# Bias of a spectral layer written into a PSUM bank by ScalarE; one copy in place of two for the inverse stage

## The chip, the cores and the metric

The kernel runs on one core of a Trainium2 chip. The metric is the device time of one launch in microseconds (us). Engines are named as in the profile: PE is TensorE's matmul, PEld its weight load, DVE is VectorE, ACT is ScalarE, POOL is GpSimd, SP is the engine that issues most DMAs.

## The reference, cut to what matters

Eight sequences of 2496 rows by 256 columns go through a spectral layer, and the result, 19968 tokens, through a top-1 mixture of eight experts.

```python
X = np.fft.rfft(x, axis=1)
Yr = Xr @ w_r - Xi @ w_i + b_r
Yi = Xr @ w_i + Xi @ w_r + b_i
Yr = np.sign(Yr) * np.maximum(np.abs(Yr) - lam, 0.0)     # Yi the same
y = np.fft.irfft(Yr + 1j * Yi, n=2496, axis=1)
...
expert_idx = np.argmax(y @ w_gate, axis=1)
ye = np.maximum(xe @ w1[e], 0.0) @ w2[e]
out = gate_w * ye          # softmax weight of the chosen expert
```

## The kernel before, in words

The transform of 2496 points is done in two factors, 39 and 64. Of the 39 columns of frequencies only 20 are needed (k1 = 0 to 19), and two of them make a slot, so a sequence has 10 slots and the eight sequences 80. A slot goes through the following steps; each is a method of the class.

- `fwd_a` (L295) does the first factor for a whole sequence: products into a bank (`pa`), a copy to `ae`, a DMA to a scratch in DRAM. `turn` (L310) reads a slot back with the axes turned.
- `fwd_b` (L317) does the second factor of one slot into the bank `pb`; `halves` (L327) splits the result into a high and a low part, `sh` and `sl`, and their sum. ACT does `re` (L334), `sh` (L335) and the `sh` of the sum (L339).
- `mix` (L343) is the complex product with w_r + i w_i as three real products of six matmuls each. The first of the three goes to the bank `pk`, and ACT copies it to `k` (L357). After a `yield` the other two go to the two halves of one bank, `pm`, which has a single buffer: first a bf16 matmul of ones with the three-way split bias (L361, 512 columns, `start=True`), then twice six products (L351) onto it. DVE adds `k` to both halves and writes `v` (L365).
- `shrink` (L369) is the soft threshold: ACT writes `r` (L373), DVE `y` (L379).
- `inv_b` (L386) does the first factor of the inverse: four fp32 products, each of two instructions in the trace, into the bank `pv`, and two ACT copies (L396) that scatter it into `z`, one per half of the 256 columns. `z` holds for each of 64 rows 40 numbers next to each other, four of them per slot.
- `inv_a` (L399) does the other factor, in groups: `pz`, the split `zh` and `zl`, `py`, and a copy to `yb`. `route` (L588) chooses the expert and scatters the rows to DRAM, as generators that `tick` steps on, mostly short DVE work.

The loop over the slots is in `spectral` (L423). In the slot loop the order on PE, SP, ACT and DVE is the order in which the code is written (`manual_schedule`); before the loop PE and SP are in written order, and ACT and DVE are ordered by a planner. Each engine takes its instructions strictly in order. In slot `it` the loop issues `fwd_b` and `halves` of the next slot, `shrink` of the last, and `mix` of this one. In slots 2 to 5 of a sequence other than the first ("turning" slots) it also issues `inv_a` of the sequence before; in the other slots `inv_b`. What stands ahead of `k` on ACT differs: in slots that are not turning, of sequences 0 to 6, it is `re`, `sh`, `r`, the `sh` of the sum and the two `z` copies; in turning slots `zh` and `ae` in place of the `z` copies; in the last sequence (`late`) the first half of `mix` is issued ahead of the `z` copies.

`pk` and `py` share a pool tag (`yo`) with two buffers, so a later `py` waits until ACT has copied `k`. `load_bias` (L200) issues six small DMAs on POOL, `split_bias` (L276) splits them in three on DVE. `keep_warm` (L543) issues products of zeros. After the loop come the last sequence's `inv_a`, and then the experts, which take the larger part of the time.

Of the kernel before, what the change touches and what calls it, by code (L numbers as in the profile page):

```python
# [10 lines left out]
F32 = mybir.dt.float32  # L11
# [9 lines left out]
NA, NB = 39, 64  # L21
# [3 lines left out]
D = 256  # L25
# [12 lines left out]
def constants(nb):  # L38
    n1 = np.arange(NA)
    n2 = np.arange(NB)  # L40
    k2 = np.arange(NB)
    fa = np.zeros((117, 120))
    fe = np.zeros((78, 120))
    ga = np.zeros((120, 117))
    for j in range(3):
        for k1 in range(K1):
            ph = 2 * np.pi * ((n1 * k1) % NA) / NA
            c, r = j * 40 + 2 * k1, slice(j * 39, (j + 1) * 39)
            for q, v in enumerate((np.cos(ph), -np.sin(ph))):
                fa[j::3, (2 * k1 + q) * 3 + j] = v  # L50
                if j < 2:
                    fe[j::2, (2 * k1 + q) * 3 + j] = v
            f = (1 if k1 == 0 else 2) / S
            ga[c, r] = f * np.cos(ph)
            ga[c + 1, r] = -f * np.sin(ph)
    bm = np.zeros((128, K1, 128))
    bi = np.zeros((128, K1, 128))
    for k1 in range(K1):
        k = k1 + NA * k2
        s = np.where(k > S // 2, -1.0, 1.0)  # L60
        th = 2 * np.pi * ((n2[:, None] * k[None, :]) % S) / S
        c, z = np.cos(th), np.sin(th)
        bm[:64, k1, :64] = c
        bm[64:, k1, :64] = z
        bm[:64, k1, 64:] = -z * s
        bm[64:, k1, 64:] = c * s
        live = (((k != 0) & (k != S // 2)) * s)[:, None]
        bi[:64, k1, :64] = c.T
        bi[64:, k1, :64] = -z.T * live
        bi[:64, k1, 64:] = z.T  # L70
        bi[64:, k1, 64:] = c.T * live
    cap = TT + nb * S
    nt = (nb * S + E * (TT - 1)) // TT
    p = np.arange(117)
    g = np.arange(G)
    n2o = p[:, None] // NA + 3 * g[None, :]
    tok = NB * (p[:, None] % NA) + n2o
    ok = n2o < NB
    ids = np.where(ok[:, None, :], tok[:, None, :] + S * np.arange(nb)[None, :, None], OOB)
    score = np.broadcast_to((8.0 - np.arange(E))[None, None, :], (117, G, E)) * ok[:, :, None]  # L80
    base = np.broadcast_to((np.arange(E) * cap + TT)[None, :], (128, E))
    ltri = (p[:, None] < p[None, :]).astype(np.float64)
    tcol = np.stack([np.arange(128.0), np.arange(128.0) - 1, np.where(np.arange(128) == 0, 1.0, 0.0),
                     np.arange(128.0), np.arange(128.0) + 128], 1)
    return {
        "c_fa": fa.astype(np.float32),
        "c_fe": fe.astype(np.float32),
        "c_ga": ga.astype(np.float32),
        "c_bm": bm.astype(np.float32),
        "c_bi": bi.astype(np.float32),  # L90
        "c_ids": np.ascontiguousarray(ids.astype(np.int32)),
        "c_score": np.ascontiguousarray(score.astype(np.float32)),
        "c_base": np.ascontiguousarray(base.astype(np.float32)),
        "c_ltri": ltri.astype(np.float32),
        "c_tcol": tcol.astype(np.float32),
    }


class Kernel:
# [243 lines left out]
    def mix(self, b, s):  # L343
        nc = self.nc
        sh, sl = self.ss.pop((b, s))

        def product(nm, slot, to, first=True, last=True):
            i = 0
            for c in range(2):
                for a, ww in ((sh, self.wh), (sh, self.wl), (sl, self.wh)):  # L350
                    nc.tensor.matmul(to, a[:, c, slot, :], ww[nm][:, c, :], start=first and i == 0, stop=last and i == 5)  # L351
                    i += 1

        pk = self.psi.tile([128, 512], F32, tag="yo", name="pk")
        product("r", 2, pk[:, :D])
        k = self.w.tile([128, D], F32, tag="k", name="k")
        nc.scalar.copy(k, pk[:, :D])  # L357
        self.mark_row(k)
        yield
        p = self.psf.tile([128, 2, D], F32, tag="m", name="pm", bufs=1)  # L360
        nc.tensor.matmul(p.rearrange("p r d -> p (r d)"), self.ones_b, self.bias3[:117], start=True, stop=False)  # L361
        product("d", 0, p[:, 1, :], False, False)
        product("s", 1, p[:, 0, :], False)
        u = self.w.tile([128, 2, D], F32, tag="v", name="v")
        nc.vector.tensor_add(u, p, k.unsqueeze(1).broadcast_to((128, 2, D)))  # L365
        self.mark_row(u)
        self.us[b, s] = u
# [18 lines left out]
    def inv_b(self, b, s):  # L386
        nc = self.nc
        y = self.ys.pop((b, s))
        p = self.psi.tile([128, 512], F32, tag="u", name="pv", bufs=4).rearrange(
            "p (c a r n) -> p c a r n", c=2, a=2, r=2)  # L390
        for kp in range(2):
            for c in range(2):
                nc.tensor.matmul(p[:, c, kp, :, :], y[:, kp, c * 128:(c + 1) * 128], self.bi[:, 2 * s + kp, :],
                                 start=True, stop=True)
        for c in range(2):
            nc.scalar.copy(self.z[:, c, 0:NB, 4 * s:4 * s + 4].rearrange("p n a -> p a n"),  # L396
                           p[:, c].rearrange("p a r n -> p (a r) n"))

    def inv_a(self, b, i):  # L399
        nc = self.nc  # L400
# [20 lines left out]
                self.jobs.append(self.route(b, g // GH, self.yb))  # L421

    def spectral(self, fwd):  # L423
        nb = self.nb
        self.t1s, self.pbs, self.ss, self.us, self.ys, self.hl = {}, {}, {}, {}, {}, {}
        self.jobs, self.rows = [], []
        pairs = [(q, g) for q in range(6) for g in ((0, 2) if q < 5 else (0,))]
# [1 line left out]
        n = len(todo)  # L429
        self.keep_warm(18)  # L430
        self.split_bias()
        for i in pairs:
            self.fwd_a(0, *i)
        self.load_weights()
# [16 lines left out]
        first, loads, back = ({i: [] for i in range(n)} for _ in range(3))  # L451
# [15 lines left out]
        for it in range(n):  # L467
            b, s = todo[it]
# [25 lines left out]
            if late and not turning:  # L494
                next(mix)
            if not turning:
                inverse()
            if not late and not turning:
                next(mix)
            for a in first[it]:  # L500
                self.fwd_a(*a)
            if turning:
                next(mix)
# [544 lines left out]
```

## Time and profile before

| | |
|---|---|
| median of 3 runs | 1521.19 us (1520.15 to 1521.5) |
| profiled execution, its own time | 1522.23 us |
| its span | 1520.4 us |
| busy, PE / DVE / ACT / POOL | 98% / 73% / 62% / 29% |
| slot loop | from 31 us to 573 us of the span |

Times in the profile are microseconds from the start of the span. A row of the timeline gives start, duration, engine, line, operation, what is written and read, and in brackets how long the engine had been idle and which engine released it. Matmuls overlap in the array, so the spacing of their starts, not their duration, is what one costs. Durations of ACT and DVE overlap the next one by about a tenth of a microsecond as well.

### The profile page before, as it was taken

The numbers are of one execution on the slowest core, as the hardware profiler recorded it, in microseconds if no ns is written. First come the engines' busy times: TensorE is split into PE (matmuls) and PEld (weight loads), VectorE is DVE, ScalarE is ACT, GpSimd is POOL, SyncE is SP. The second block draws the span as 40 slices with busy tenths as digits, with TensorE's granted clock in tenths as the row PEclk, the third lists the DMA queues.
The fourth block names the chain that finished last, engine by engine and source line by source line (L and its number), as shares of the span: only waits on it lengthen the run. The fifth ranks groups of instructions, "written<-read, shape, count | busy, mean of one in ns | idle before, by whom it ended". The sixth has DMA issues, their size and how long they took to land. (4 is left out here: it accounts for less than half of the span.)

```text
span 1520.4 us, 29861 instructions
## 1 busy us (share of the span) xinstructions
PE 1496.1 (98%) x9367; PEld 1313.4 (86%) x9367; DVE 1105.4 (73%) x2412; ACT 943.0 (62%) x2008; POOL 439.6 (29%) x527
## 2 busy tenths in 40 slices
PE   8999999999999999999999999999999999999997
PEld 4789899998989988888888888888888888998997
DVE  4678687777777987676766667666666666788885
ACT  2677777777777767455555555555555555676764
POOL 1101524435261635611221221122122112232232
PEclk9999999999999999999999999999999999999999
DMA  8953545546362314452232413322323243555421
GB/s 247 278 156 111 174 144 148 156 144 181 113 195 86 113 33 156 116 133 53 57 91 50 112 41 73 83 56 70 71 56 104 44 105 98 145 143 153 100 49 28
DMA packets 191518, 169.69 MB, mean 112 GB/s; under 512 B 117525, under 2 KB 159881, under 8 KB 191354
## 3 DMA queue, kind: packets, MB, share of 16 engines
q1 hardware_dynamic: 171390, 123.48, 31.9%
q0 software_dynamic: 19712, 43.75, 8.7%
q8 instruction: 76, 1.25, 0.4%
q14 instruction: 88, 0.72, 0.2%
q10 hardware_dynamic: 252, 0.50, 0.1%
HBM read 171.51 MB, written 66.37 MB: 156 GB/s over the span
## 5 line engine op out<-in xcount | busy, mean ns | idle before, releaser
L965 PE MATMUL po<-h,hh 128*128 128x512 f32 x1312 | 453.7, 393 | 0.0
L909 ACT ACTIVATE hh<-ph 128x512 fp32r<-128x512 f32 x328 | 196.1, 598 | 209.6 <-PE ph L904 189.2
L962 PE MATMUL po<-h,hl 128*128 128x256 f32 x1148 | 321.2, 280 | 0.0
L910 DVE SCALAR_TENSOR_TENSOR hl<-ph,hh 128x512 fp32r<-128x512 f32 x328 | 226.2, 691 | 125.8 <-ACT hh L909 117.9
L939 POOL DMA_INDIRECT out<-o,xr x116 | 139.3, 1201 | 501.1 <-DVE o L937 495.1
L904 PE MATMUL ph<-xh,l 128*128 128x512 f32 (+1 forms) x800 | 281.2, 351 | 1.0 <-DVE l L834 1.0
L904 PE MATMUL ph<-xh,h 128*128 128x512 f32 (+1 forms) x800 | 281.4, 352 | 0.3 <-ACT h L833 0.2
L904 PE MATMUL ph<-xl,h 128*128 128x512 f32 (+1 forms) x800 | 280.7, 351 | 0.0
L965 PEld LDWEIGHTS po<-h,hh 128*128 128x128 f32 x1312 | 238.4, 188 | 43.0 <-ACT hh L909 0.2
L962 PEld LDWEIGHTS po<-h,hl 128*128 128x128 f32 x1148 | 215.8, 188 | 6.0
L654 POOL DMA_INDIRECT xs_dram<-yb,pos x176 | 177.8, 1010 | 70.1 <-issue 35.3
L904 PEld LDWEIGHTS ph<-xh,l 128*128 128x128 f32 x800 | 151.3, 189 | 22.7 <-DVE l L834 1.6
L936 ACT ACTIVATE part<-po,xr 128x256 f32<-128x256 f32 x152 | 72.2, 475 | 156.5 <-PE po L965 156.5
L904 PEld LDWEIGHTS ph<-xl,h 128*128 128x128 f32 x800 | 151.3, 189 | 20.2
L904 PEld LDWEIGHTS ph<-xh,h 128*128 128x128 f32 x800 | 151.3, 189 | 19.9 <-ACT h L833 0.8
L937 DVE SCALAR_TENSOR_TENSOR o<-po,xr,part 128x256 f32<-128x256 f32 x152 | 73.3, 482 | 111.2 <-ACT part L936 108.9
L379 DVE SCALAR_TENSOR_TENSOR y<-v,r 64x256 f32<-64x256 f32 x320 | 133.8, 418 | 6.8 <-ACT r L373 1.6
L834 DVE TENSOR_TENSOR l<-r,h 128x512 fp32r<-128x512 f32 x200 | 128.1, 686 | 5.0 <-ACT h L833 3.5
L849 DVE TENSOR_TENSOR h<-r,h 128x512 fp32r<-128x512 f32 x200 | 127.8, 684 | 2.0 <-ACT h L848 1.3
L833 ACT CAST h<-r 128x512 fp32r<-128x512 f32 x200 | 112.2, 616 | 2.9 <-DMA r<-moe_w 2.8
L848 ACT CAST h<-r 128x512 fp32r<-128x512 f32 x200 | 112.3, 617 | 1.6 <-DMA r<-moe_w 1.6
L939 POOL DMA_INDIRECT out<-o,row x36 | 63.8, 1773 | 142.7 <-DVE o L937 136.6
(178 smaller groups left out, 2832.7 us busy)
## 6 DMA issues: line engine op xcount, KB each, us to landing
r<-moe_w SPq DMA_DIRECT2D x106, 512.0 KB
r<-moe_w SPq DMA_DIRECT2D x376, 128.0 KB
spec_dram<-ae SPq DMA_DIRECT2D x88, 240.0 KB
t<-spec_dram SPq DMA_DIRECT2D x160, 128.0 KB
x<-x SPq DMA_DIRECT2D x40, 384.0 KB
xq<-xs_dram SPq DMA_DIRECT2D x116, 128.0 KB
xq<-xs_dram SPq DMA_DIRECT2D x72, 64.0 KB
x<-x SPq DMA_DIRECT2D x35, 84.0 KB
```

Source lines behind the costliest of these rows:

```text
L379: nc.vector.scalar_tensor_tensor(out=y[q * 64:q * 64 + 64, kp, :], in0=u[h, q, :], scalar=LAM, in1=r[h, q, :], op0=ALU.add, op1=ALU.min)
L654: i = nc.gpsimd.indirect_dma_start(out=self.xs[:, :], out_offset=bass.IndirectOffsetOnAxis(ap=pos[:n, g:g + 1], axis=0), in_=y[:n, g, 0:XW ...
L833: nc.scalar.copy(hi[:, c, s], v)
L834: nc.vector.tensor_sub(lo[:, c, s], v, hi[:, c, s])
L848: nc.scalar.copy(hi[:, s, :], v)
L849: nc.vector.tensor_sub(lo[:, s, :], v, hi[:, s, :])
L904: nc.tensor.matmul(p[:, i, :], a[:, c, f * 128:(f + 1) * 128], v[:, c, :], start=m == 0, stop=m == 5)
L909: nc.scalar.activation(hh[:, s, :], p, AF.Relu)
L910: nc.vector.scalar_tensor_tensor(out=hl[:, s, :], in0=p, scalar=0.0, in1=hh[:, s, :], op0=ALU.max, op1=ALU.subtract)
L939: i = nc.gpsimd.indirect_dma_start(out=self.out[:, :], out_offset=bass.IndirectOffsetOnAxis(ap=at[h], axis=0), in_=o[:, h, :], in_offset=N ...
L962: nc.tensor.matmul(p[:, :D], hl[:, f - 1, hs], w2[:, f - 1, 0, :], start=False, stop=False)
L965: nc.tensor.matmul(p, hh[:, f, hs], w2[:, f].rearrange("p a d -> p (a d)"), start=f == 0, stop=f == 7)
```

## The change

The columns of the table `bi` are interleaved, so that `pv` can be laid out with the four numbers of a slot next to each other, and one ACT copy moves both halves into `z` in runs of four numbers (16 bytes). Each product of `inv_b` then writes its 128 columns as 64 pairs, with a gap of two numbers after each pair. The bias is summed once, ahead of the first `fwd_a`, by one matmul into the bank `pm` with `start=True`, and DVE copies it to a tile `biasf`. In each slot ACT copies `biasf` (128 x 512) into the bank `pm`, ahead of `k` on ACT, and all twelve products of the second half of `mix` add to it; none of them has `start=True`.

```diff
-        bi[:64, k1, :64] = c.T
-        bi[64:, k1, :64] = -z.T * live
-        bi[:64, k1, 64:] = z.T
-        bi[64:, k1, 64:] = c.T * live
+        bi[:64, k1, 0::2] = c.T
+        bi[64:, k1, 0::2] = -z.T * live
+        bi[:64, k1, 1::2] = z.T
+        bi[64:, k1, 1::2] = c.T * live
...
         product("r", 2, pk[:, :D])
+        p = self.psf.tile([128, 2, D], F32, tag="m", name="pm", bufs=1)
+        nc.scalar.copy(p.rearrange("p r d -> p (r d)"), self.biasf)
         k = self.w.tile([128, D], F32, tag="k", name="k")
         nc.scalar.copy(k, pk[:, :D])
         self.mark_row(k)
         yield
-        p = self.psf.tile([128, 2, D], F32, tag="m", name="pm", bufs=1)
-        nc.tensor.matmul(p.rearrange("p r d -> p (r d)"), self.ones_b, self.bias3[:117], start=True, stop=False)
         product("d", 0, p[:, 1, :], False, False)
         product("s", 1, p[:, 0, :], False)
...
-            "p (c a r n) -> p c a r n", c=2, a=2, r=2)
+            "p (c n a r) -> p c n a r", c=2, a=2, r=2)
         for kp in range(2):
             for c in range(2):
-                nc.tensor.matmul(p[:, c, kp, :, :], y[:, kp, c * 128:(c + 1) * 128], self.bi[:, 2 * s + kp, :],
+                nc.tensor.matmul(p[:, c, :, kp, :], y[:, kp, c * 128:(c + 1) * 128], self.bi[:, 2 * s + kp, :],
                                  start=True, stop=True)
-        for c in range(2):
-            nc.scalar.copy(self.z[:, c, 0:NB, 4 * s:4 * s + 4].rearrange("p n a -> p a n"),
-                           p[:, c].rearrange("p a r n -> p (a r) n"))
+        nc.scalar.copy(self.z[:, :, 0:NB, 4 * s:4 * s + 4], p.rearrange("p c n a r -> p c n (a r)"))
...
         self.keep_warm(18)
         self.split_bias()
+        p = self.psf.tile([128, 512], F32, tag="m", name="pm0", bufs=1)
+        nc.tensor.matmul(p, self.ones_b, self.bias3[:117], start=True, stop=True)
+        self.biasf = self.f.tile([128, 2 * D], F32, name="biasf")
+        nc.vector.tensor_copy(self.biasf, p)
         for i in pairs:
             self.fwd_a(0, *i)
```

## Rows read from the trace of the kernel before

**Rows 1.** The page, busy time by engine: us, share of the span, number of instructions.

```profile
PE 1496.1 (98%) x9367; PEld 1313.4 (86%) x9367; DVE 1105.4 (73%) x2412; ACT 943.0 (62%) x2008; POOL 439.6 (29%) x527
```

**Rows 2.** Busy time in one stretch, the last 13 slots of the loop: length, then busy us of PE, PEld, DVE, ACT, POOL with the instructions, granted clock, DMA share, GB/s.

```profile
485.00:572.00 87.00, 84.43 (x680) 79.39 (x680) 76.62 (x241) 61.71 (x148) 40.66 (x64) 1.00 0.27 80
```

**Rows 3.** What PE waited for from 30 to 600 us: waiting line, what released it, total us, times, longest.

```profile
PE pb L323 <- DMA t<-spec_dram: 1.6, 1, 1.6
...
PE py L418 <- ACT k L357: 0.8, 1, 0.8
```

**Rows 4.** Groups of instructions by line over the whole span: shapes, count, busy us, mean ns of one, idle before.

```profile
L833 ACT CAST h<-r 128x512 fp32r<-128x512 f32 x200 | 112.2, 616 | 2.9 <-DMA r<-moe_w 2.8
...
L396 ACT COPY z<-pv 128x256 f32<-128x256 f32 x160 | 92.9, 707 | 1.5 <-PE pv L393 1.5
...
L335 ACT CAST sh<-pb 128x512 fp32r<-128x512 f32 x80 | 47.4, 592 | 0.0
...
L361 PE MATMUL pm<-bias,ones_b 117*128 117x512 bf16 x80 | 30.9, 387 | 0.3 <-DVE v L365 0.3
```

**Rows 5.** Timeline of ACT in one slot, slot 1 of sequence 4, to the first row of the next slot.

```profile
302.76 0.37 ACT L334 COPY re<-pb 128x256 f32<-128x256 f32 x1 [1.84 <-PE pb L323]
303.03 0.59 ACT L335 CAST sh<-pb 128x512 fp32r<-128x512 f32 x1
303.51 0.74 ACT L373 ACTIVATE r<-v,nlam 128x512 f32<-128x512 f32 x1
...
304.43 1.17 ACT L396 COPY z<-pv 128x256 f32<-128x256 f32 x2
305.35 0.46 ACT L357 COPY k<-pk 128x256 f32<-128x256 f32 x1
...
307.76 0.37 ACT L334 COPY re<-pb 128x256 f32<-128x256 f32 x1 [1.48 <-PE pb L323]
```

**Rows 6.** Timeline of PE in the same slot: the bias product, and the second and third of the twelve products after it.

```profile
304.98 0.38 PE L361 MATMUL pm<-bias,ones_b 117*128 117x512 bf16 x1
...
305.31 0.28 PE L351 MATMUL pm<-wld,sh 128*128 128x256 f32 x1
305.43 0.28 PE L351 MATMUL pm<-whd,sl 128*128 128x256 f32 x1
```

**Rows 7.** Timeline, the bias product on PE and `k` on ACT in other slots that are not turning: slots 5 and 9 of sequence 0, slots 6 and 7 of sequence 3 (with the `pv` products of the latter), slot 0 of sequence 4.

```profile
61.37 0.46 ACT L357 COPY k<-pk 128x256 f32<-128x256 f32 x1
61.86 0.38 PE L361 MATMUL pm<-bias,ones_b 117*128 117x512 bf16 x1
...
83.95 0.38 PE L361 MATMUL pm<-bias,ones_b 117*128 117x512 bf16 x1
84.32 0.46 ACT L357 COPY k<-pk 128x256 f32<-128x256 f32 x1
...
275.60 0.45 ACT L357 COPY k<-pk 128x256 f32<-128x256 f32 x1
276.28 0.38 PE L361 MATMUL pm<-bias,ones_b 117*128 117x512 bf16 x1
...
281.27 1.05 PE L393 MATMUL pv<-bi,y 128*128 128x128 f32 x8
282.16 0.38 PE L361 MATMUL pm<-bias,ones_b 117*128 117x512 bf16 x1
282.88 0.45 ACT L357 COPY k<-pk 128x256 f32<-128x256 f32 x1
...
299.49 0.46 ACT L357 COPY k<-pk 128x256 f32<-128x256 f32 x1
299.98 0.38 PE L361 MATMUL pm<-bias,ones_b 117*128 117x512 bf16 x1
```

**Rows 8.** Timeline of a turning slot, slot 3 of sequence 4: `k` on ACT, the second `py` after it and the bias product on PE.

```profile
319.46 0.38 ACT L357 COPY k<-pk 128x256 f32<-128x256 f32 x1
...
320.45 0.29 PE L418 MATMUL py<-zh,gh 120*117 120x272 f32 x1
...
320.83 0.39 PE L361 MATMUL pm<-bias,ones_b 117*128 117x512 bf16 x1
```

**Rows 9.** Timeline: the bias product and `k` in slot 7 of sequence 6, and the bias product four slots later, in slot 1 of sequence 7.

```profile
490.28 0.38 PE L361 MATMUL pm<-bias,ones_b 117*128 117x512 bf16 x1
...
491.88 0.43 ACT L357 COPY k<-pk 128x256 f32<-128x256 f32 x1
...
509.43 0.38 PE L361 MATMUL pm<-bias,ones_b 117*128 117x512 bf16 x1
```

**Rows 10.** Timeline of the start: the last of POOL's six bias DMAs, the first products of `fwd_a`, SP's issues of `ae` to DRAM, the first round of the bias split on DVE, and the first reads of a slot.

```profile
5.37 0.48 POOL L205 DMA_DIRECT2D bias<-b_i  x1
...
7.73 3.60 PE L299 MATMUL pa<-x,far 117*120 117x512 f32 x8
...
11.04 8.73 SPq L308 DMA_DIRECT2D spec_dram<-ae  x11
...
14.56 0.41 DVE L281 CAST b<-bias 128x512 bf16<-128x512 f32 x1
...
15.21 0.67 DVE L284 TENSOR_TENSOR bias<-bias,b 128x512 f32<-128x512 f32 x1
...
22.80 2.57 SPq L314 DMA_DIRECT2D t<-spec_dram  x4
```

More of the change, by code (lines that the diff above doesn't have):

```diff
@@ L350, in product @@
                 for a, ww in ((sh, self.wh), (sh, self.wl), (sl, self.wh)):
-                    nc.tensor.matmul(to, a[:, c, slot, :], ww[nm][:, c, :], start=first and i == 0, stop=last and i == 5)
+                    nc.tensor.matmul(to, a[:, c, slot, :], ww[nm][:, c, :], start=first and i == 0, stop=last and i == 5,
+                                     skip_group_check=not first)
                     i += 1
@@ L423, in spectral @@
     def spectral(self, fwd):
-        nb = self.nb
+        nc, nb = self.nc, self.nb
         self.t1s, self.pbs, self.ss, self.us, self.ys, self.hl = {}, {}, {}, {}, {}, {}
```

## The prediction, as put on record

> **What bounds the kernel now.** I read the page's busy times first. PE is busy for 98% of the span [rows 1], so a saving on PE counts, and so does every wait that PE is given. Next I asked what PE waited for in the slot loop, since the change is made there: one wait for a DMA of 1.6 us, one of 0.8 us for `k`, and little else [rows 3]. So PE sets the time of the loop, and ACT and DVE follow it. Only the last 13 slots differ: there DVE is busy for 76.6 of 87.0 us [rows 2], and PE has little left over it. Last I read the timeline slot by slot for one question: how far is ACT behind PE at the point where the change makes PE wait for ACT?
>
> **What the edit takes from PE.** The bias product starts at 304.98 and the second of the twelve products at 305.31 [rows 6]; the third follows the second after 0.12 us, so the bias product costs 0.33 - 0.12 = 0.21 us. There are 80 [rows 4]: 16.8 us if nothing waits.
>
> **What it puts on ACT.** One copy of 128 x 512 from SBUF into PSUM. No row shows that direction. The nearest are 592 ns (PSUM to SBUF) and 616 ns (SBUF to SBUF) for the same shape [rows 4]; I take 0.60 us until it is done, with ends of 0.45 and 0.74 (`r`, [rows 5]). Until the next instruction can start I take 0.50 us (`sh` to `r` is 0.48 [rows 5]). The Trainium skill (page "ScalarE: Activation LUTs", section "Step-by-step: what each stage is for") says that ScalarE writes faster to PSUM than to SBUF; that would lower the 0.60, and no row here shows by how much.
>
> **What it takes from ACT.** Two `z` copies, of 0.707 us mean [rows 4], which together hold ACT from 304.43 to 305.35, 0.92 us [rows 5]. One copy of twice the size, four numbers at a time: I take the contiguous 128 x 512 rate, 0.48 us to the next start, since `k`, as large as one `z` copy and contiguous, takes 0.46 against 0.707. The other end is no gain, 0.92. ACT's total hardly changes (0.50 more, 0.44 less). Its order does matter.
>
> **The new wait.** The bias copy stands on ACT directly ahead of `k`, behind `z`, and PE's twelve products now wait for it. Behind them on PE are `pb` of the next slot, and so `re`, `sh` and everything after; ACT is idle 1.8 us before `re` and waits for `pb` [rows 5], so a slot that is late makes the next late by as much. Where two `z` copies stand ahead, `k` starts now at z + 0.92; the bias copy will start at z + 0.48 and end at z + 1.08, that is `k` + 0.16; with 0.06 us for the release, PE can go on at `k` + 0.22. Now I compare this, slot by slot, with the time at which PE reaches the bias product today:
>
> - Slot 1 of a sequence: 305.35 + 0.22 - 304.98 = 0.59 us late; less the 0.21 saved, 0.38 us lost [rows 5, 6]. Six sequences (1 to 6): +2.3.
> - Slot 7, where an exponential of the routing delays ACT: 282.88 + 0.22 - 282.16 = 0.94 late, 0.73 lost [rows 7]. Sequences 1 to 5: +3.65. Slot 8 is taken as even.
> - Slots 0, 6 and 9: 299.49 + 0.22 - 299.98 is negative, and so is 275.60 + 0.22 - 276.28 [rows 7]. No wait, 0.21 gained: 6 + 6 + 5 slots, -3.6.
> - Turning slots: the bias copy begins where `k` does, 319.46, and ends at 320.06; PE comes at 320.83 [rows 8]. 24 slots, -5.1. But `k` ends 0.50 later, at 320.34, and the `py` at 320.45 needs its bank: 0.05 us to spare, and none where `k` is late already, as in the one wait of 0.8 us [rows 3, 8]. I add 1.0, with ends 0 and 3.
> - Sequence 0: slots 2 to 5 gain (61.37 against 61.86), 7 to 9 lose 0.38 each (84.32 + 0.22 - 83.95 - 0.21) [rows 7]. The first slot loses about 1. What has gathered before slot 8 falls into the DMA wait of 1.6 us [rows 3]; slots 8 and 9 remain: +0.8.
>
> Sequences 1 to 6 come to 2.3 + 3.65 - 3.6 - 5.1 + 1.0 = -1.8.
>
> **The last slots.** From slot 7 of sequence 6 ACT is far behind PE, because `r` waits for DVE. That slot loses 491.88 + 0.22 - 490.28 - 0.21 = 1.6 us [rows 9]. After it a ring closes: bias copy, twelve products, `pb`, `re`, `sh`, `r`, `sh` of the sum, bias copy. From the products to the next `re` takes 307.76 - 304.98 - 0.21 = 2.57 us, from `re` to where `z` stands 1.67 [rows 5, 6], the bias copy with its release 0.66: 4.90 us, and 5.38 with a `z` copy ahead. Four slots, two of each kind, need 20.6 us; PE does them in 509.43 - 490.28 = 19.15 today [rows 9]. So 1.4 more, 3.0 with the first. Slots 2 to 6 of sequence 7 give back 5 x 0.21. In slots 7 to 9 DVE sets the pace [rows 2], and only the last bias copy shows, about +0.5. Together +2.5.
>
> **The start.** PE's order is the written one, and the new matmul `pm0` stands ahead of the first `fwd_a`. It needs the whole bias split, which DVE does today from 14.56 on, in between. The last bias DMA is issued at 5.85. When it lands no row tells: after 5.85 and before 14.56. By SP's writes, whose last issue ends at 19.77 and whose readers start at 22.80, 3.0 us from issue to landing: 8.9. Two rounds of 1.32 us (14.56 to 15.88) and a short third make 3.3 us: `pm0` at 12.2, where `fwd_a` begins at 7.73 today [rows 10]. That is 4.5 us later. Part of it comes back, since by then more of x has landed and the writes share the DMA engines with fewer loads. I take +2.5, with ends 0 and +9 (a landing at 14.56).
>
> **Sum.** -1.8 + 0.8 + 2.5 + 2.5 = +4.0 us on the profiled execution's 1522.2: 1526.2. It lies 1.0 above the median, so 1525 us for the median.
>
> **Rivals.**
> 1. *The copy is hidden and PE keeps its saving.* 80 x 0.21 less the start's 2.5: 1507 us. For it: ACT idles before every `re`. Against it: that idle time lies before `re`, and the copy is at the end of ACT's chain. It decides if `z` and the bias copy together take under 0.55 us in slot 1; I have 1.08. Chance 0.14.
> 2. *The single `z` copy costs as much as the pair.* Then the bias copy ends 0.44 us later: some 20 slots that already wait lose 8.8, the ten with a margin of 0.27 lose 0.17 each, the last slots about 1: +11.5, 1537 us. For it: no row has runs of four. Chance 0.12.
> 3. *The products of `inv_b` slow down*, because they write pairs with gaps. Today eight of them start 0.111 us apart (281.27 to 282.16 [rows 7]). At double the spacing, 640 x 0.111 = +71 us: 1596 us. No row has such an output. The Trainium skill speaks against the change here: "PSUM — Partial Sum Buffer", section "Specifications (TRN2)", says that any non-contiguous pattern slows matmuls significantly. [...] Chance 0.05.
> 4. *The start costs nothing*, because the bias lands early and the DMAs make up the rest: 1522.5 us, no difference. Chance 0.14.
>
> **How the numbers follow.** My forecast has 0.55. Within 0.2% (3 us, about what can be told from no change) lie 1518.2 to 1524.2. Of the 0.55 the larger part, 0.39, is slower, 0.13 the same, 0.03 faster. With the rivals: slower 0.39 + 0.12 + 0.05 = 0.56, the same 0.13 + 0.14 = 0.27, faster 0.17. The bounds of the bias copy (25 waiting slots by 0.15 us, 4 us) and of the start (-2.5 to +6.5) give the forecast its own range, 1518 to 1533. For 8 in 10 I take 1512 to 1540, which leaves out rival 3 and rival 1 in its full size.
>
> **What would show it.** Right: PE's list of waits has the products of `pm` released by ACT's `pm` copy, about 0.6 us in each slot 1 and 0.9 in each slot 7, none in slots 0, 6, 9 and in turning slots; `z` rows of about 0.6 us in one piece; the first `fwd_a` near 12 us and the first `pb` near 29. Wrong: a list of waits without ACT's copy, or `pv` products more than 0.111 us apart, or a first `fwd_a` still near 8 us.

## The result and the profile after

The changed kernel takes 1537.67 us (median of 4 runs, 1536.68 to 1540.2) against 1521.35 us for the kernel before on the same chip: ratio 1.0106, 95% interval 1.009 to 1.0122. It is slower by 16.3 us. The forecast was slower by about 4. The profiled executions differ by the same amount: the span is 1536.5 us against 1520.4.

The page's busy times say at once that PE did not lose by working more.

```profile
PE 1487.4 (97%) x9286; PEld 1306.2 (85%) x9288; DVE 1106.4 (72%) x2413; ACT 934.1 (61%) x2008; POOL 437.7 (28%) x527
```

PE is busy for 8.7 us less than in [rows 1], and the span is 16.1 us longer, so PE waits for about 25 us more. The list of what PE waited for, from 0 to 620 us (total us, times, longest), names the waits:

```profile
PE pm L351 <- ACT pm L358: 15.6, 22, 2.2
PE pm L432 <- DVE bias L282: 10.1, 1, 10.1
PE py L417 <- ACT k L360: 3.3, 4, 1.5
PE pb L323 <- DMA t<-spec_dram: 2.4, 1, 2.4
...
PE py L417 <- ACT yb L418: 1.8, 2, 1.3
```

One wait of 10.1 us is the summed bias at the start. Twenty-two waits of 15.6 us together are the products of `mix` waiting for ACT's copy of the bias. `py` waiting for `k` has grown from 0.8 us [rows 3] to 3.3.

The groups by line (count, busy us, mean ns of one, idle before) give the price of each new or changed operation:

```profile
L394 PE MATMUL pv<-bi,y 128*128 128x128 f32 x640 | 85.3, 277 | 1.3 <-DMA bi<-c_bi 1.2
...
L351 PE MATMUL pm<-whd,sh 128*128 128x256 f32 x160 | 52.2, 326 | 15.6 <-ACT pm L358 15.6
...
L358 ACT COPY pm<-biasf 128x512 f32<-128x512 f32 x80 | 48.4, 605 | 0.0
...
L396 ACT COPY z<-pv 128x512 f32<-128x512 f32 x80 | 47.2, 596 | 2.1 <-PE pv L394 2.1
```

The bias copy takes 605 ns, the single `z` copy 596 ns, and the `pv` products, which now write pairs with gaps, 277 ns.

To see where the time went I followed one instruction that every slot has, ACT's `re`, and took its start in both kernels, slot by slot. The view of the tile `re` has the first and the last start in the loop, first for the kernel before and then for the changed one:

```profile
L334 ACT COPY re<-pb x80: 356/372/453, 28.1 to 558.3; 128x256 f32<-128x256 f32 x80
```

```profile
L334 ACT COPY re<-pb x80: 353/372/376, 37.6 to 577.8; 128x256 f32<-128x256 f32 x80
```

The first `re` is 9.5 us late and the last 19.5. Taken apart at the slots that the prediction named, the delay grows like this (us); a slot ends with the `re` that follows its twelve products:

| stretch | predicted | measured |
|---|---|---|
| start, to the first `re` | +2.5 | +9.5 |
| slot 0 of sequence 0 | about +1, absorbed later | +3.0 |
| rest of sequence 0 | +0.8 | +1.1 |
| sequences 1 to 6, up to slot 6 of the last | -1.8 | +0.9 |
| the last slots, to the last `re` | +2.5 | +5.0 |
| after the loop | 0 | -3.4 |
| sum | +4.0 | +16.1 |

**The start.** The timeline of the changed kernel's start, as in [rows 10] (start, duration, engine, line, what is written and read, and in brackets the idle time and its releaser):

```profile
5.36 0.48 POOL L205 DMA_DIRECT2D bias<-b_i  x1
...
13.23 0.43 DVE L281 CAST b<-bias 128x512 bf16<-128x512 f32 x1 [10.82 <-DMA bias<-b_i]
...
16.55 0.28 DVE L282 COPY bias<-b 1x512 bf16<-1x512 bf16 x1
...
16.89 0.59 PE L432 MATMUL pm<-bias,ones_b 117*128 117x512 bf16 x1 [10.11 <-DVE bias L282]
17.26 10.70 PE L299 MATMUL pa<-x,far 117*120 117x512 f32 x20
...
27.80 1.02 PE L299 MATMUL pa<-x,fer 78*120 78x512 f32 x2
...
32.69 2.58 SPq L314 DMA_DIRECT2D t<-spec_dram  x4
...
36.43 1.13 PE L323 MATMUL pb<-bm,t 128*128 128x128 f32 x8 [2.43 <-DMA t<-spec_dram]
```

DVE stands idle until the last bias DMA has landed, at 13.2 us. The split then runs until 16.83, `pm0` follows at 16.89, and the first `fwd_a` begins at 17.26, 9.5 us later than in [rows 10]. The readers of `spec_dram` begin at 32.69 against 22.80, 9.9 later. Nothing of the delay came back on the way. In the kernel before, the same products of `fwd_a` began at 7.73 and went on like this:

```profile
11.96 5.38 PE L299 MATMUL pa<-x,far 117*120 117x512 f32 x12 [0.63 <-DMA x<-x]
17.32 1.09 PE L299 MATMUL pa<-x,fer 78*120 78x512 f32 x2
```

From the first of the twenty to the pair behind them it takes 9.6 us with a wait of 0.63 us for x; the changed kernel has no such wait and takes 10.5. The reason is the clock. Busy time in windows of the start (length, busy us of PE, PEld, DVE, ACT and POOL with the instructions, granted clock, DMA share, GB/s):

```profile
18.00:19.00 1.00, 1.00 (x3) 0.35 (x2) 0.20 (x1) 0.00 (x0) 0.00 (x0) 0.50 0.00 0
...
22.00:24.00 2.00, 2.00 (x6) 0.80 (x5) 0.69 (x1) 0.87 (x2) 0.00 (x0) 1.00 0.60 165
...
40.00:44.00 4.00, 2.93 (x14) 2.64 (x13) 1.35 (x3) 1.76 (x5) 0.00 (x0) 0.50 0.95 241
44.00:48.00 4.00, 3.96 (x18) 3.96 (x19) 0.69 (x1) 0.29 (x1) 0.00 (x0) 0.50 1.00 265
```

After PE's idle time of 10.1 us the first products of `fwd_a` run at a granted clock of 0.50, the 1.2 GHz level. The profiles of e2, e7, e8 and e9, which have the same long wait, show this level there too; those of e1 and e3, without it, do not. The first of these rows shows that no DMA was moving between 18 and 19 us: no load of x was outstanding then, and the writes waited for PE.

**Slot 0.** The last two of these rows are slot 0, at 0.50 too. The kernel before runs part of this slot at that level as well, as two of its windows show:

```profile
33.00:34.00 1.00, 1.00 (x7) 0.83 (x6) 0.83 (x2) 0.51 (x3) 0.00 (x0) 0.67 0.75 250
34.00:35.00 1.00, 1.00 (x11) 1.00 (x10) 0.52 (x2) 0.30 (x2) 0.00 (x0) 1.00 0.86 274
```

There the clock comes back within the bias product and the first of the twelve. In the changed kernel PE idles 1.11 us for the bias copy at this place, and the low level lasts through all twelve products and most of the next `pb`, to 48.5 us. Of the 3.0 us that slot 0 lost, 1.2 are the wait (from the first `pk` product to the first of the twelve 2.73 us against 1.52) and 1.8 the longer time at the low level. That the wait makes this time longer is not shown. The kernel before, run again on another chip (e6, below), has no wait there. It reaches its bias product at 34.25, after which the windows show:

```profile
36.00:37.00 1.00, 1.00 (x6) 1.00 (x6) 0.00 (x0) 0.00 (x0) 0.00 (x0) 0.50 0.74 211
37.00:38.00 1.00, 1.00 (x10) 1.00 (x9) 0.51 (x1) 0.00 (x0) 0.00 (x0) 0.92 0.90 242
```

So there, too, the low level lasts until the last of the twelve has started, and that kernel's slot 0 takes 5.1 us from `re` to `re`, against 4.0 in the first run and 7.0 in the changed kernel. A part of the 1.8 us can be the difference between two executions.

**A slot of the loop.** Slot 1 of sequence 4, to be compared with [rows 5, 6]:

```profile
317.82 0.60 ACT L396 COPY z<-pv 128x512 f32<-128x512 f32 x1
318.30 0.61 ACT L358 COPY pm<-biasf 128x512 f32<-128x512 f32 x1
318.82 0.40 ACT L360 COPY k<-pk 128x256 f32<-128x256 f32 x1
...
318.96 0.39 PE L351 MATMUL pm<-whd,sh 128*128 128x256 f32 x1 [0.42 <-ACT pm L358]
```

From `z` to the bias copy there are 0.48 us, the copy lasts 0.61, and PE goes on 0.05 us after it, having idled 0.42 us. Idle time is counted from the modelled end of the product before, about 0.16 us after the next one could have started (products of 0.28 us, 0.12 apart [rows 6]), so the 0.42 stands for the 0.6 that the prediction looked for in slot 1, and the 0.74 of each slot 7 for its 0.9.

### The profile page after: what moved, and what is told of

It reads as the page before. It is cut to its first block, busy times and chain, and to the rows that moved or that the text cites. A ratio compares the mean times of both kernels' runs of the same rounds, so it can differ in the third digit from the quotient of the medians.

```text
span 1536.5 us, 29735 instructions
## 1 busy us (share of the span) xinstructions
PE 1487.4 (97%) x9286; PEld 1306.2 (85%) x9288; DVE 1106.4 (72%) x2413; ACT 934.1 (61%) x2008; POOL 437.7 (28%) x527
```

## The experiments

The runs were made in three sets on three chips: e1 to e4, e5 to e8, and e9 to e11. On each of them the kernel before itself is slower than in the first runs, whose chip is not on record, at 1556 to 1560 us, so a run is compared with others of its set or by its ratio. No run leaves any computation out.

| run | kernel | median us | before, same set | ratio (95%) |
|---|---|---|---|---|
| e1 | changed, summed bias later | 1560.86 | 1559.82 | 1.0014 (1.0001 to 1.0026) |
| e2 | changed, copy early in the slot | 1570.19 | 1559.82 | 1.0062 (1.0041 to 1.0083) |
| e3 | both | 1557.76 | 1559.82 | 0.9991 (0.9979 to 1.0002) |
| e4 | `z` part alone | 1553.74 | 1559.82 | 0.9965 (0.9951 to 0.9979) |
| e5 | both, placement by slot | 1551.94 | 1559.20 | 0.995 (0.9929 to 0.997) |
| e6 | before, one run for its profile | 1560.04 | 1559.20 | one run |
| e7 | changed kernel again | 1573.35 | 1559.20 | 1.0082 (1.0063 to 1.0101) |
| e8 | bias part alone | 1593.86 | 1559.20 | 1.0223 (1.0206 to 1.024) |
| e9 | before, with the start alone | 1566.78 | 1556.18 | 1.0067 (1.0043 to 1.0091) |
| e10 | as e5 | 1548.37 | 1556.18 | 0.9944 (0.9924 to 0.9963) |
| e11 | as e4 | 1552.92 | 1556.18 | 0.9982 (0.9971 to 0.9994) |

My theory after the result was that two placements make the loss: `pm0` ahead of the first `fwd_a`, and the bias copy behind `z` on ACT. The rivals: the delay of the start is hidden or given back by the end; PE's products slow down for another reason; the copy costs the same wherever it stands.

**The summed bias later (e1).** `pm0` and its copy go behind the first sequence's `fwd_a`.

```diff
-        p = self.psf.tile([128, 512], F32, tag="m", name="pm0", bufs=1)
...
         for i in pairs:
             self.fwd_a(0, *i)
+        p = self.psf.tile([128, 512], F32, tag="m", name="pm0", bufs=1)
+        nc.tensor.matmul(p, self.ones_b, self.bias3[:117], start=True, stop=True)
+        self.biasf = self.f.tile([128, 2 * D], F32, name="biasf")
+        nc.vector.tensor_copy(self.biasf, p)
```

> The changed kernel with the bias product pm0 and the copy to biasf behind the eleven first-factor products of sequence 0 instead of ahead of them. Theory (the start costs 10 us because PE stands in front of pm0 until the bias has landed and is split, and slot 0 then runs at half clock): 1526 to 1528 us, first pb at 26 to 27 us. Rival (DMA makes the start up later and the loop's waits are the whole loss): above 1534 us.

Measured: the ratio falls from the changed kernel's 1.0082 (e7, on another chip) to 1.0014, 0.68% or 10.6 us. So e1 gained a little more than expected: 1526 to 1528 us are ratios of 1.003 to 1.004. The timeline of its start:

```profile
7.17 5.62 PE L299 MATMUL pa<-x,far 117*120 117x512 f32 x12
...
18.34 0.38 PE L434 MATMUL pm<-bias,ones_b 117*128 117x512 bf16 x1 [0.81 <-DVE bias L282]
...
25.52 1.13 PE L323 MATMUL pb<-bm,t 128*128 128x128 f32 x8 [1.63 <-DMA t<-spec_dram]
...
32.76 0.58 PE L351 MATMUL pm<-whd,sh 128*128 128x256 f32 x1 [1.11 <-ACT pm L358]
```

`pm0` waits 0.81 us in place of 10.1, and `pb` begins at 25.52 in place of 36.43. The 1.11 us in slot 0 stay. What is left, 0.14%, is what the rest of the change loses on that chip.

**The copy early in the slot (e2), and both edits (e3).** The copy goes behind `sh`, ahead of `r` and of `z` or `zh`; e3 has the later start as well.

```diff
-        p = self.psf.tile([128, 2, D], F32, tag="m", name="pm", bufs=1)
-        nc.scalar.copy(p.rearrange("p r d -> p (r d)"), self.biasf)
+        p = self.pm
...
                 next(half)
+            self.pm = self.psf.tile([128, 2, D], F32, tag="m", name="pm", bufs=1)
+            nc.scalar.copy(self.pm.rearrange("p r d -> p (r d)"), self.biasf)
```

> The changed kernel with the bias copy at the head of the slot on ACT, right behind sh and ahead of r, instead of behind z and ahead of k; the start as in the changed kernel. Theory (PE's products wait for the copy because of its place in ACT's order): the 22 waits of 15.6 us go, 1522 to 1525 us. Rival (the half microsecond on ACT costs as much wherever it stands, through r, y and the rest): above 1533 us.

> Both edits: pm0 behind the first-factor products, the copy at the head of the slot. Theory (two separate costs that add, and a saving of 0.21 us per slot underneath): 1506 to 1513 us, faster than both kernels. Rival (the saving on PE is given back elsewhere, for instance to DVE in the last slots): 1516 to 1521 us.

Measured: 1.0062 and 0.9991. Both fell short of what I expected: 1522 to 1525 us are ratios of 1.000 to 1.002, so e2 lies between its theory and its rival, and e3 came out at its rival's number (1516 to 1521 us, 0.996 to 1.000), not told apart from the kernel before. The two ratios differ by 0.71%, 11 us, which is the start once more, here within one set. Against e1, e3 gains 3.1 us by moving the copy, though the two intervals just overlap. From 100 to 480 us the list of PE's waits of e3 has no wait for the bias copy any more. Another is at its head:

```profile
PE pk L351 <- ACT yb L417: 4.8, 9, 0.6
```

In a turning slot the early copy stands ahead of `zh` and `yb` on ACT, and `pk` shares its two buffers with `py`, so it waits for `yb`. The copy's place therefore matters in both directions: behind `z` it holds up PE in slots 1 and 7, and ahead of `zh` it does so in the turning slots.

**Placement by slot (e5, e10).** Early in slots that are not turning; ahead of `k`, as in the change, in those that are; later start.

```diff
+        if b and 2 <= s < 6:
+            self.seed()
+        p = self.pm
...
+    def seed(self):
+        self.pm = self.psf.tile([128, 2, D], F32, tag="m", name="pm", bufs=1)
+        self.nc.scalar.copy(self.pm.rearrange("p r d -> p (r d)"), self.biasf)
...
+            if not turning:
+                self.seed()
```

> As e3_both, but in turning slots the bias copy stays where the change has it, ahead of k; at the head of the slot only in the other slots. Theory (at the head of a turning slot the copy delays yb and zh, and PE waits for them at pk and py; ahead of k it costs almost nothing there): PE's waits for yb in the turning slots go, and the loop to slot 6 of sequence 6 ends 12 to 16 us ahead of the changed loop's own gain or loss, that is 8 to 12 us earlier than in the kernel before; time 1.0 to 1.5% under the changed kernel with its start mended. Rival (the waits in turning slots come from the scatter DMAs of the rows and not from ACT's order): no better than e3_both.

> The mixed placement once more, on the same chip as the z part alone. Theory (the bias copy, well placed, keeps something of the 0.21 us of each product): 3 to 8 us under the z part alone. Rival (the 0.21 us of each product is spent again by the copy's own waits): within 3 us of it.

Measured: 0.995 and, on the next chip, 0.9944. PE's waits of e10 from 100 to 480 us:

```profile
PE py L422 <- ACT k L361: 2.1, 7, 0.6
PE py L422 <- issue: 1.0, 1, 1.0
```

Neither the waits for the bias copy nor those for `yb` are left in this stretch. This version beats both kernels, the kernel before by 0.5%. Against e1 it is 0.6% better and not the 1.0 to 1.5% that I expected.

**The `z` part alone (e4, e11).** The kernel before with the interleaved table and the single copy; the bias stays a product.

```diff
...
-                nc.tensor.matmul(p[:, c, kp, :, :], y[:, kp, c * 128:(c + 1) * 128], self.bi[:, 2 * s + kp, :],
+                nc.tensor.matmul(p[:, c, :, kp, :], y[:, kp, c * 128:(c + 1) * 128], self.bi[:, 2 * s + kp, :],
...
-        for c in range(2):
-            nc.scalar.copy(self.z[:, c, 0:NB, 4 * s:4 * s + 4].rearrange("p n a -> p a n"),
-                           p[:, c].rearrange("p a r n -> p (a r) n"))
+        nc.scalar.copy(self.z[:, :, 0:NB, 4 * s:4 * s + 4], p.rearrange("p c n a r -> p c n (a r)"))
```

> The kernel before with the interleaved table and the single z copy alone; the bias stays a product. Theory (ACT is not on PE's path here, pairs cost PE nothing): 1519 to 1522 us, pv products still 0.111 us apart, z about 0.60 us. Rival (writing pairs with gaps slows the products of inv_b): above 1530 us.

> The z part alone, beside the mixed placement. Both theories: 4 to 8 us under the kernel before, as on the other chip. They differ in the distance to the mixed placement only.

Measured: 0.9965 and 0.9982, a small gain both times. My first expectation had none (1519 to 1522 us), and in the second set the gain is 3.3 us, less than the 4 to 8 expected; where it comes from was not tried. In the second set the mixed placement is 4.55 us under it, and the two intervals of the ratio do not overlap (0.9963 and 0.9971). So the bias copy, well placed, does keep a part of PE's saving, 4.55 of 16.8 us in these medians.

**The bias part alone (e8)**, the change with the old table and the pair of `z` copies.

```diff
...
-        nc.scalar.copy(self.z[:, :, 0:NB, 4 * s:4 * s + 4], p.rearrange("p c n a r -> p c n (a r)"))
+        for c in range(2):
+            nc.scalar.copy(self.z[:, c, 0:NB, 4 * s:4 * s + 4].rearrange("p n a -> p a n"),
+                           p[:, c].rearrange("p a r n -> p (a r) n"))
```

> The changed kernel once more, beside the others on one chip. Both theories: 1.0 to 1.2% above the kernel before, first pb near 36 us.

> The changed kernel without its z part: two z copies with the old table, the bias as in the change. Theory (z's single copy, 0.44 us shorter on ACT and ahead of the bias copy, shortens every wait): PE's waits for the bias copy grow from 15.6 us by 9 to 12 us, time 9 to 12 us above the changed kernel. Rival (the waits do not depend on z, since r and the sum set ACT's pace): within 3 us of the changed kernel.

Measured: the changed kernel again is 0.82% over the kernel before, less than the 1.0 to 1.2% expected, and e8 is 20.5 us over it, about twice what I expected. Groups by line of the changed kernel (e7), the copy and the first weight load behind it, and then the same of e8:

```profile
L358 ACT COPY pm<-biasf 128x512 f32<-128x512 f32 x80 | 48.8, 610 | 0.0
...
L351 PEld LDWEIGHTS pm<-whd,sh 128*128 128x128 f32 x160 | 30.6, 191 | 33.7 <-ACT pm L358 23.5 <-ACT z L396 6.1 <-issue 2.9
```

```profile
L358 ACT COPY pm<-biasf 128x512 f32<-128x512 f32 x80 | 53.9, 674 | 0.0
...
L351 PEld LDWEIGHTS pm<-whd,sh 128*128 128x128 f32 x160 | 30.2, 189 | 54.3 <-ACT pm L358 52.2 <-ACT sh L339 1.0
```

The weight load waits 20.6 us more, as much as the whole difference. The copy starts 0.44 us later, as reckoned, and is 64 ns longer in the mean. In slots with a pair ahead it lasts longer by more than that:

```profile
317.91 1.15 ACT L397 COPY z<-pv 128x256 f32<-128x256 f32 x2
318.83 0.71 ACT L358 COPY pm<-biasf 128x512 f32<-128x512 f32 x1
```

There it takes 0.71 us, against 0.61 behind the single copy, and is done 0.54 us later in all. That is more than the margins by which slots 0 and 9 (0.27 us) and 6 (0.46) had escaped a wait [rows 7], so they lose as well. The `re` rows of e8 and e7 show it: in most sequences slots 1 and 7 take 0.57 us longer, slots 0 and 8 about 0.4, and slots 6 and 9 about 0.2. Why the copy itself is longer behind the pair was not tried.

**The start alone (e9).** The kernel before plus the summed bias matmul and DVE's copy ahead of the first `fwd_a`, whose result nobody uses.

```diff
+        p = self.psf.tile([128, 512], F32, tag="m", name="pm0", bufs=1)
+        self.nc.tensor.matmul(p, self.ones_b, self.bias3[:117], start=True, stop=True)
+        self.biasf = self.f.tile([128, 2 * D], F32, name="biasf")
+        self.nc.vector.tensor_copy(self.biasf, p)
```

> The kernel before, unchanged but for the summed bias matmul and its copy by DVE ahead of the first products of fwd_a (the copy's result is not used; the slots keep their bias product and the pair of z copies). Theory (the start is the larger part of the loss, and nothing of it comes back): the first pb 9 to 10 us later than in the kernel before on the same chip, and a time 9 to 12 us above it. Rival (the loop or the DMA waits take the delay back): under 5 us.

Measured: 10.6 us over the kernel before of its set. Its timeline:

```profile
16.69 0.59 PE L433 MATMUL pm<-bias,ones_b 117*128 117x512 bf16 x1 [9.09 <-DVE bias L282]
...
37.48 1.13 PE L323 MATMUL pb<-bm,t 128*128 128x128 f32 x8 [2.74 <-DMA t<-spec_dram]
```

`pb` begins at 37.48, 10.5 us later than in the one profile of the kernel before on such a chip (27.02 in e6), and the time is 10.6 us longer; little or nothing of the delay comes back later. This isolates the largest term: four lines of code ahead of `fwd_a` cost 10.6 us on that chip, and taking them from there gave back about the same (e1 against e7, e3 against e2).

**The kernel before again (e6)**, with its profile, to see why these chips are slower.

> The kernel before once more, for its trace on the same chip as the others of this call. Theory (what the first experiments lost after slot 0 of sequence 7 is late instructions on that chip and hits every kernel): if its time is near 1560 us, its trace shows engines idle with no releaser after 490 us; if it is near 1521 us, none. Rival (it is the edits): the trace to 600 us is as in the first profile at either time.

Its span is 1558.2 us, 37.8 longer than in the first profile. Busy time in three windows of e6, and in the same windows of the first profile:

```profile
480.00:560.00 80.00, 72.72 (x573) 69.02 (x572) 64.40 (x200) 52.40 (x132) 26.62 (x42) 0.96 0.26 76
560.00:640.00 80.00, 66.85 (x446) 60.81 (x446) 52.99 (x161) 47.01 (x110) 36.76 (x50) 0.91 0.30 96
640.00:700.00 60.00, 52.17 (x260) 42.89 (x259) 35.02 (x83) 26.04 (x49) 22.27 (x25) 0.94 0.41 109
```

```profile
480.00:560.00 80.00, 78.17 (x642) 74.76 (x641) 70.95 (x225) 57.29 (x140) 30.41 (x49) 1.00 0.25 75
560.00:640.00 80.00, 76.35 (x476) 66.09 (x476) 59.29 (x175) 49.01 (x110) 51.65 (x64) 1.00 0.40 126
640.00:700.00 60.00, 60.00 (x304) 51.08 (x303) 42.99 (x69) 34.76 (x64) 11.56 (x10) 1.00 0.50 120
```

PE is busy for 22.8 us less in these 220 us, more than half of the 37.8. The stretch behind it, 700 to 1500 us, keeps PE busy for 798.9 us against 798.7. So the larger part of the difference lies at the end of the loop and just behind it, in a kernel that does not have the change.

## Why the prediction was right in its direction and too small in its size

The changed kernel is slower, as forecast, and its 1537.67 us lie inside the 1512 to 1540 given for 8 in 10, but outside the 1518 to 1533 that the forecast's own terms were given. The wide range held because it left room for the rivals. That rival 2 stands at 1537 is a coincidence: its mechanism did not occur. The mechanism of the new wait was right; sizes were off, most of all at the start.

- **The start failed, and it is the mis-sized term.** I took +2.5 us, with ends 0 and +9, from two steps. The landing of the last bias DMA was put at 8.9 us, by the 3.0 us that SP's writes take; it was 13.2, so POOL's small DMA took 7.4 us from its issue at 5.85. And I let two of 4.5 us "come back"; none did. `fwd_a` began 9.5 us late and `pb` 10.0. Part of what I had counted on, that more of x would have landed by then, was so, but it saved 0.63 us only, and the low clock after PE's idle time cost more. This one term misses by 7.0 us of the 12.1 that the whole sum misses. e9 and e1 show it from both sides (+10.6 and -10.6 us). The measured +9.5 lies just past the end of +9 that I had kept for it; by the prediction's own working that end, a landing at 14.56, is 14.56 + 3.3 - 7.73 = 10.1 before anything comes back.
- **Slot 0 failed in size.** I had "about 1" and let the DMA wait of slot 8 absorb it. The wait was 1.1 to 1.2 us as reckoned. The further 1.8 us are the longer time at the low clock level, of which I had no term; e6 shows that it varies between executions without any such wait. The DMA wait in slot 7 of this sequence absorbed only 0.7 us: it was 1.6 [rows 3], and at the same place the changed kernel still waits 0.9.
- **The stall formula held.** `k` + 0.22 minus PE's arrival gave 0.38 us lost in slot 1 and 0.73 in slot 7; the `re` rows of both kernels give 0.47 and 0.79. In sequences 1 to 5 slots 0, 6, 8 and 9 gained 0.20 to 0.24 us, against 0.21 predicted (slot 8 had been taken as even). In sequence 0, slot 4 lost 0.4 where a gain was predicted, and slot 6, which has no term there, 0.2; in these two PE waits 0.75 and 0.43 us for the table `bi`.
- **The turning slots gave less.** Slots 3 and 5 gained 0.18 us, near the predicted 0.21; slot 2 gained nothing, and slot 4 went from -1.2 to +1.4 us, depending on the sequence. The spread of slot 4 is the term "`py` waits for `k`, 1.0 with ends 0 and 3". The kernel before has such a wait in slot 4 of sequence 2, and the changed kernel has three, in slot 4 of sequences 3, 4 and 5; the first row is of the kernel before, the second, the longest of the three, of the changed kernel:

```profile
190.04 0.38 PE L418 MATMUL py<-zh,gh 120*117 120x272 f32 x1 [0.80 <-ACT k L357]
...
273.75 0.39 PE L417 MATMUL py<-zh,gh 120*117 120x272 f32 x1 [1.48 <-ACT k L360]
```

The others are 1.02 and 0.18 us, so the term came to 1.9 (2.7 less 0.8) in these sequences; the fourth wait of the list, 0.6, is in sequence 7. Together this turned the -1.8 us of sequences 1 to 6 into +0.9 (24 times 0.21 is 5.0, where the prediction has 5.1). Why `k` is late in some sequences and not in others was not settled.

- **The last slots had the right mechanism.** From the ring I took 3.0 us for its five slots, and the `re` rows give 3.4; slots 2 to 6 of sequence 7 gave back 1.1, about as predicted. Slot 7 then lost 2.7 us by the `re` rows, where I had 0.5 for the rest, which makes +5.0 by the end of the loop. I had nothing given back afterwards; 3.4 us were, so the net, 1.6, lies under the forecast of 2.5. What gives them back was not traced.
- **The new operations cost what was taken:** the copy 605 ns (0.60), the `z` copy 596 (0.48 to the next start, as measured). The Trainium skill's page "ScalarE: Activation LUTs" (section "Step-by-step: what each stage is for") has ScalarE write faster to PSUM than to SBUF; the 605 ns lie between the 592 and the 616 of [rows 4], so this trace shows no more than 11 ns of such a gain for this shape.

**The rivals.** The hidden copy (1507) fell with PE's 15.6 us of waits for it. The single `z` copy as dear as the pair fell with 596 ns. With the pair itself in its place, e8, the price is 20.5 us and not the 11.5 that I gave the rival: slots lose their margin by more than I had counted, and the bias copy is longer there. The slowed `inv_b` products fell with 277 ns each before and after, at the same spacing (0.112 us in the median of either trace). The Trainium skill's page "PSUM — Partial Sum Buffer" (section "Specifications (TRN2)") warns of any pattern that is not contiguous. The page "Advanced Engine Details and Errata" of the Trainium skill (section "Memory Cachelines") has the same warning and beside it the advice that every two consecutive elements should be contiguous, which the pairs are. For such pairs this trace shows no slowing. The free start fell with the 10.1 us.

## What to carry to other kernels

On an engine that runs in written order, ask of every instruction put ahead of the first real work when its data land, and read that from the transfer's own kind (queue, size) and not from another's. Bound such a wait by the latest landing that the rows allow, and give nothing back for it without naming a row that will be short. When work moves from the bounding engine to one that follows it, the gain is decided by the place of the new instruction in the other queue: here the same copy cost 0.47 us in one kind of slot and gained 0.2 in another, and choosing its place per slot, with the summed bias moved behind `fwd_a`, turned a loss of about 1% into a gain of 0.5%, of which the single `z` copy alone gives 0.2 to 0.35%.

## What was not expected of the hardware

Six DMAs of 1 KB issued on POOL at the start land late: the last is issued at 5.85 and awaited until 13.2. The changed kernel's view of DMA issues (operation, count, KB each, median us from issue to landing) has for three of them:

```profile
bias<-b_i POOLq DMA_DIRECT2D x3, 1.0 KB, 7.1
```

A read that had to follow SP's writes began 3.0 us after the last of them [rows 10], and that was the figure I had used.

How long PE stays at the 1.2 GHz level in slot 0 differs between executions: the changed kernel leaves it at 48.5 us, 1.9 after the last of the twelve products has started, the kernel before at 33.7 in one profile, ahead of most of them, and at 37.1 in the other (e6), 0.1 after the start of the last. e1, with the same wait of 1.11 us as the changed kernel, leaves it at 36.0, 0.7 us after the last of its twelve has started. What decides it stays open.

Three chips ran the kernel before 2.3 to 2.5% slower than it ran at first. In the one profile taken of it there, 22.8 us of the difference are idle PE between 480 and 700 us. For some of these waits the trace names no releaser; what they are stays open.
